# The first linear layer of the state-read tokens in seven half products

## The chip, the cores and the metric

The kernel runs on one core of a Trainium2 chip. Its time is the device time of one execution in microseconds, the median of several runs. Before the change it is 203.69 us (three runs, 203.05 to 204.18).

## The reference

The input x is 8 batches x 8 heads x 512 rows x 64, the state 8 x 8 x 32 x 64. Attention is taken both ways, and the result goes through a feed-forward layer with SILU:

```python
scores = scale * np.matmul(x, state.transpose(0, 1, 3, 2))
a = np.exp(scores); a /= a.sum(-1, keepdims=True) + 1e-09
xread = np.matmul(a, state)
scores2 = scale * np.matmul(state, x.transpose(0, 1, 3, 2))
a2 = np.exp(scores2); a2 /= a2.sum(-1, keepdims=True) + 1e-09
sread = np.matmul(a2, x)
attn = np.concatenate([xread, sread], axis=2)
# rows of attn, 512 wide (8 heads x 64), are the tokens
h = tokens @ w_in            # 512 -> 2048
out = silu(h) @ w_out        # 2048 -> 512
```

Each batch gives 544 tokens: 512 from `xread` and 32 from `sread`. The change concerns the 8 x 32 = 256 tokens of `sread`, the state-read tokens.

## The kernel before

The order of all work is written out by hand: each engine does its instructions in the order in which the code names them, and waits where an operand or a buffer isn't ready. A batch b = 0..7 has two layers. G1 gives h for 16 tiles of 128 features and ScalarE turns each into g with SILU (`emit_G1`, L549). G2 multiplies g by `w_out_sb`. From batch 1 on G2 is done by class `Unit` (L608) in seven products of half the size instead of eight (Strassen's scheme in Winograd's form): g is cut in two halves of features (lo, hi) and of tokens, `w_out_sb` in B11 to B22, and VectorE makes sums of both (`sums1` to `sums4`, D1 to D4 in `wt`). `u.mm(p, k)` is step k of 8 of product p, two matmuls of 128x256. Products 1, 6 and 5 add up in the PSUM bank `al`, and their intermediate sums are copied out (`kept[0]` by VectorE, `keep` by ScalarE); products 7, 2, 4, 3 each use the one bank `be`, which VectorE must have read before the next of them starts. POOL makes two of the sums of blocks; a block (i, c) is a quarter of the output of one batch. `out_half` stores half of it.

In the loop over batches (L906) G1 of batch b and products 1 and 7 of its G2 alternate (`early`, L924), then come products 2, 6, 4, 5, 3 (`units`, L1011), among which G1 of the next batch begins. Batch 7 has no next batch. There, the state-read tokens follow. Their attention sums were made in batches 1, 4 and 6 (`sread`) and moved by DMA to `xs`; `place_xm` (L450) brings them to `xmT`, [128, 2 halves of 128 tokens, 4 slices of the 512 inputs, 128 tokens], in 8 copies of 64x256 on VectorE (L958). Their G1 is the branch `b == B` of `emit_G1`: for each of 16 tiles of features four matmuls of 128x256 (L558) into a bank with the tag "h1", of which there are two, and a SILU of 128x256 (L568). Two tiles come ahead of product 2 (L990), the others are spread over products 6, 4, 5 and 3 (L1016). `sread_diff` (L752) then takes one difference of g on VectorE within product 3.

`sread_out_product` (L695) is G2 of the state-read tokens, again in seven products, and the end of the kernel: p1, p7, p6, p2, p5, p4, p3 with 8 matmuls of 128x256 each (p3 in two parts of 128x128 matmuls, 8 each). p1, p6 and p5 add up in one bank. Four stores leave on the queues of SP and ScalarE.

The banks of PSUM: `bank` (L77) hands out four in turn, `psH` two ("h1"), `psO` two ("o0" for `be`, "o1" for `al`). `x_f` (L109) are two buffers for x in f32, needed until the last batch of x is converted to bf16 by POOL; `x_nat` holds two tiles of 4 KB per partition.

Of the kernel before, what the change touches and what calls it, by code (L numbers as in the profile page):

```python
# [18 lines left out]
B = 8  # L19
H = 8  # L20
# [22 lines left out]
def kernel(  # L43
# [12 lines left out]

    pers = ctx.enter_context(tc.tile_pool(name="pers", bufs=1))
    xpool = ctx.enter_context(tc.tile_pool(name="xpool", bufs=2))
    xtpool = ctx.enter_context(tc.tile_pool(name="xtpool", bufs=2))
    att = ctx.enter_context(tc.tile_pool(name="att", bufs=2))  # L60
    epool = ctx.enter_context(tc.tile_pool(name="epool", bufs=6))
# [44 lines left out]
    xT = {}  # L106


    x_f = [pers.tile([128, H, 4, D], FP32, name=f"x_f{i}") for i in range(2)]  # L109

    def load_x(b, h0=0, nh=H, eng=nc.gpsimd):
        eng.dma_start(
# [45 lines left out]
    def copy(eng, dst, src):  # L158
        if eng is nc.scalar:
            nc.scalar.activation(dst, src, func=COPY, bias=0.0)  # L160
        else:
            eng.tensor_copy(dst, src)  # L162
# [337 lines left out]

    def g_tile(k):
        b, ft = divmod(k, NFT)
        if b == B:
            if ft == 0:
                gh[b, 0] = gpool.tile([128, NFT, 256], BF16, tag="g", name="g")
            gt[k] = gh[b, 0][:, ft, :]
        else:
            if ft % 8 == 0:
                gh[b, ft // 8] = gpool.tile([128, 8, 512], BF16, tag="g", name="g")
            gt[k] = gh[b, ft // 8][:, ft % 8, :]  # L510

    h_ps = {}

# [34 lines left out]

    def emit_G1(k):  # L549
        b, ft = divmod(k, NFT)  # L550
        if b < B:
            g1_half(k, 0)
            g1_half(k, 1)
            ps = h_ps.pop(k)
        else:
            ps = psH.tile([128, 512], FP32, tag="h1", name="h1")
            for kt in range(4):
                nc.tensor.matmul(  # L558
                    ps[:, 0:256],
                    w_in_sb[:, kt, ds(128 * ft, 128)],  # L560
                    xmT[:, :, kt].rearrange("p t n b -> p t (n b)"),
                    start=(kt == 0),
                    stop=(kt == 3),
                    skip_group_check=True,
                )
        n = 512 if b < B else 256
        g_tile(k)
        nc.scalar.activation(gt[k], ps[:, 0:n], func=SILU, bias=0.0)  # L568

    def G2(b, tt, ft):  # L570
        if ft == 0:
# [18 lines left out]
    def sub(eng, dst, a, c):  # L590
        eng.tensor_tensor(dst, a, c, op=SUB)  # L591

    def add(eng, dst, a, c):
        eng.tensor_tensor(dst, a, c, op=ADD)  # L594
# [97 lines left out]
            nc.sync.dma_start(out_sread[ds(512, 32), ds(4 * tt, 4), :], o[:])  # L692


    def sread_out_product():  # L695
        g = gh[B, 0]
        half = lambda e, t: g[:, ds(8 * e, 8), ds(128 * t, 128)]
        a11, a21, a12, a22 = half(0, 0), half(0, 1), half(1, 0), half(1, 1)
        t8 = lambda nm: spool.tile([128, 8, 128], BF16, tag=nm, name=nm)
        s1, s2 = t8("s1"), t8("s2")  # L700
        u1, u3 = (spool.tile([128, 256], FP32, tag=nm, name=nm) for nm in ("u1", "u3"))
        o = [o1pool.tile([128, DM], FP32, tag=f"o_s{i}", name="o_s") for i in range(2)]
        al = psO.tile([128, 256], FP32, tag="o1", name="o")

        def product(left, right, to=None, first=True, c=0, n=256):
            if to is None:
                to = bank([128, 256], FP32, "o_s")
            for k in range(8):
                nc.tensor.matmul(  # L709
                    to[:, 0:n],  # L710
                    left[:, k],
                    right[:, k, ds(c, n)],
                    start=(first and k == 0),
                    stop=(k == 7),
                    skip_group_check=True,
                )
# [35 lines left out]
    def sread_diff():  # L752
        g = gh[B, 0]
        sub(nc.vector, g[:, 0:8, 128:256], g[:, 0:8, 0:128], g[:, 0:8, 128:256])

    done = [0]

# [148 lines left out]
    for b in range(1, B):  # L906
# [25 lines left out]
        for j in range(lead, NFT):  # L932
            upto(NFT * b + j + 1)
            if j == 8:
                u.hi = gh[b, 1]
            if j == max(lead, 5):
                if b == 1:
                    t_weights((3,), 4, 4)
                    transpose_x(3)
                u.sums3(0, 4)  # L940
                if 1 < b and m + 1 < B:
                    fetch_x(m + 1)
                if b == 2:
                    for v in range(2):
                        evict_state(v, (nc.vector, nc.gpsimd)[v], 4, 4)
            if j == 9:
                u.sums3(4, 4)
                if b == 1:
                    for v in range(2):
                        evict_state(v, (nc.vector, nc.gpsimd)[v], 2, 2)  # L950
                    t_weights((2, 4), 4, 4, nc.gpsimd)
                elif n < B:
                    norm_t(n)
                    if b in SREAD_AT:
                        spread_x(n)
# [31 lines left out]
        if 2 < b < B - 1:  # L987
            out_a()
        if n == B:
            upto(NFT * B + 2)  # L990
        if b == 1:
            for hg in range(2):
                scores(2, hg)
        for k in range(8):
            u.mm(2, k)
        if b == 2:
            made = group_a()
        add(nc.vector, u.block(0, 0), u.kept[0][:], u.be[:])
# [7 lines left out]
            out_a()  # L1006
        if 1 < b and m < B:
            exps_t(m)
        step = 0

        def units(p, leads={}):  # L1011
            nonlocal step
            for k in range(8):
                u.mm(p, k)
                if n == B and (p != 6 or k > 5):
                    upto(NFT * B + 2 + (step + 1) * (NFT - 2) // 26)  # L1016
                    step += 1
                    if (p, k) == (3, 1):
                        sread_diff()
                if n < B and k in leads:  # L1020
                    upto(NFT * n + leads[k])

# [29 lines left out]

        if b > 1:
            group_b()
        units(5, {7: 1} if b > 1 else {})
        u.keep(nc.scalar, 0, 1)
        add(nc.gpsimd, u.block(1, 1), u.kept[1][:], u.block(0, 1))
# [9 lines left out]
            transpose_x(m + 1)  # L1067
        for ft in range(NFT):
            gt.pop(NFT * b + ft)
    upto(NFT * B + NFT)  # L1070
    sread_out_product()
# [1 line left out]
_INS = ['x', 'state', 'moe_w_in', 'moe_w_out']  # L1073
# [26 lines left out]
```

## Time and profile before

| | |
|---|---|
| median of three runs | 203.69 us (203.05 to 204.18) |
| the profiled execution: its time | 203.69 us |
| its span, first to last instruction | 201.9 us |
| TensorE busy | 195.3 us, 1912 matmuls |
| VectorE, ScalarE, POOL busy | 137.6, 138.2, 72.1 us |
| granted TensorE clock, mean | 0.996 of full speed |
| G1 of the state-read tokens on TensorE | 64 matmuls of 128x256, from 175.55 to 191.6 us |
| last arithmetic instruction ends | 198.37 us |

The times in the text count from the start of the span. Line numbers (L...) are those of the kernel before unless it says otherwise. A row of a group of instructions shows line, engine, operation, tiles (out<-in), shapes and count, then busy time in us and the mean length of one in ns, then the idle time ahead of them and who ended it. A row of the view in order of time shows start, length, engine, line and operation; in square brackets the idle time before it and who ended it. A matmul's length is its passage through the array; the next one starts earlier, so that prices of matmuls are taken from starts.

### The profile page before, as it was taken

The page shows a single profiled execution, that of the slowest core. Times are in us where ns is not written, and L with a number is a line of the kernel's source. Part 1 is how long each engine was busy: PE and PEld are TensorE (multiplying, and loading weights), DVE is VectorE, ACT ScalarE, POOL GpSimd, SP SyncE. Part 2 cuts the span into 40 slices and gives each one's busy share as a digit, 9 for nine tenths or more (in the row PEclk, how much of TensorE's full clock was granted, in tenths as well). Part 3 has the DMA queues.
Part 4 walks back from the last instruction along what each step waited for, and adds up shares of the span by engine and source line. Part 5 has one row for each costly group of instructions (what it writes and reads, how often), then busy time and mean ns, then how long its engine had stood idle before and what let it go on. Part 6 is the DMA issues. An engine that isn't in the chain of part 4 may idle for free.

```text
span 201.9 us, 4650 instructions
## 1 busy us (share of the span) xinstructions
PE 195.3 (97%) x1912; PEld 130.7 (65%) x1912; DVE 137.6 (68%) x244; ACT 138.2 (68%) x245; POOL 72.1 (36%) x89
## 2 busy tenths in 40 slices
PE   7899999999999999999999999999999999999992
PEld 2444335567766676667766677668666876688881
DVE  3862655977997899388947974779369955862162
ACT  2875657889767887879787957888588168724520
POOL 8673333696534702730373034323202230002200
PEclk9999999999999999999999999999999999999998
DMA  5999999995057996494239812965142005000222
GB/s 183 194 205 206 246 263 348 211 238 120 3 147 186 238 269 123 200 273 102 52 136 281 162 27 56 259 101 29 38 196 55 13 3 208 0 3 0 102 109 104
DMA packets 40965, 28.71 MB, mean 142 GB/s; under 512 B 27376, under 2 KB 37616, under 8 KB 40944
## 3 DMA queue, kind: packets, MB, share of 16 engines
q1 hardware_dynamic: 34736, 20.65, 40.5%
q0 software_dynamic: 5920, 7.64, 18.3%
q8 instruction: 15, 0.25, 0.5%
q10 hardware_dynamic: 288, 0.13, 0.2%
q14 instruction: 6, 0.05, 0.1%
HBM read 17.43 MB, written 8.91 MB: 130 GB/s over the span
## 4 chain that ended last, share of the span: by engine, by line
PE 86%; DMA 8%; POOL 2%; DVE 1%; ACT 1%; issue 1%; POOLq 0%
PE o L646 43%; PE h L540 25%; DMA x_f<-in_x_dram 8%; PE ps_w L473 4%; PE h L558 4%; PE ps_busy L168 2%; PE o_a L577 1%; PE o L709 1%; PE o_s L709 1%; PE ps_sr L420 1%; PE o L577 1%; PE ps_xt L257 1%; PE ps_scT L336 1%; POOL w_in_sb L153 1%; PE ps_sc L310 1%
## 5 line engine op out<-in xcount | busy, mean ns | idle before, releaser
L568 ACT ACTIVATE g<-h 128x512 bf16<-128x512 f32 (+1 forms) x142 | 79.9, 573 | 34.5 <-PE h L540 23.7
L646 PEld LDWEIGHTS <-g 128*128 128x128 bf16 x560 | 54.2, 98 | 29.1 <-issue 0.5
L540 PE MATMUL h<-aT,W 128*128 128x512 bf16 x252 | 72.7, 379 | 0.1
L646 PE MATMUL o<-w_out_sb,g 128*128 128x256 bf16 x336 | 48.6, 273 | 0.1
L646 PE MATMUL o<-wt,g 128*128 128x256 bf16 x224 | 33.0, 273 | 0.0
L594 POOL TENSOR_TENSOR o_sb<-o_sb,kept 128x512 f32<-128x512 f32 x7 | 11.0, 1569 | 54.8 <-ACT o_sb L160 39.6
L540 PEld LDWEIGHTS <-W 128*128 128x128 bf16 x252 | 24.4, 98 | 8.6 <-issue 0.8
L646 PE MATMUL o<-wt,s 128*128 128x256 bf16 x224 | 27.4, 273 | 0.0
L162 DVE CAST W<-ps_w 128x512 bf16<-128x512 f32 (+1 forms) x35 | 21.7, 664 | 6.3 <-PE ps_w L473 6.3
L594 DVE TENSOR_TENSOR o_sb<-o_sb,o 128x512 f32<-128x512 f32 x14 | 9.6, 682 | 24.1 <-PE o L646 20.8
L646 PEld LDWEIGHTS <-s 128*128 128x128 bf16 x224 | 21.5, 98 | 4.3 <-issue 1.7
L160 ACT ACTIVATE W<-ps_w 128x512 bf16<-128x512 f32 (+1 forms) x31 | 16.4, 583 | 5.7 <-PE ps_w L473 5.6
L162 POOL CAST x_nat<-x_f 128x512 bf16<-128x512 f32 x24 | 16.2, 716 | 6.0 <-issue 4.1
L591 DVE TENSOR_TENSOR g<-g 128x1024 bf16<-128x1024 bf16 x15 | 11.8, 784 | 9.2 <-ACT g L568 9.2
L594 POOL TENSOR_TENSOR o_sb<-kept,o_sb 128x512 f32<-128x512 f32 x7 | 8.9, 1265 | 24.1 <-ACT o_sb L160 24.1
L160 ACT ACTIVATE o_sb<-o 128x512 f32<-128x512 f32 x15 | 8.9, 595 | 10.1 <-issue 6.8
L591 DVE TENSOR_TENSOR g<-g,s 128x1024 bf16<-128x1024 bf16 x15 | 14.1, 978 | 0.0
L162 DVE COPY kept<-o 128x512 f32<-128x512 f32 x14 | 9.6, 686 | 6.2 <-PE o L646 6.0
L366 POOL TENSOR_TENSOR an<-e,rcn 128x512 bf16<-128x512 bf16 x5 | 7.7, 1534 | 15.7 <-DVE rcn L364 15.6
L591 DVE TENSOR_TENSOR s<-g 128x512 bf16<-128x512 bf16 (+3 forms) x23 | 12.5, 571 | 0.1
L473 PE MATMUL ps_w<-w_in_sb,stT 64*32 64x512 bf16 (+1 forms) x264 | 10.2, 375 | 0.3 <-DMA w_in_sb<-in_moe_w_in_dram 0.3
L577 PEld LDWEIGHTS <-g 128*128 128x128 bf16 x64 | 5.8, 98 | 7.0 <-issue 0.8
(104 smaller groups left out, 212.7 us busy)
## 6 DMA issues: line engine op xcount, KB each, us to landing
out_dram<-o_sb SPq DMA_DIRECT2D x14, 512.0 KB, 2.7
x_f<-in_x_dram SPq DMA_DIRECT2D x6, 512.0 KB, 4.6
x_f<-in_x_dram POOLq DMA_DIRECT2D x2, 1024.0 KB, 11.6
x_f<-in_x_dram SPq DMA_DIRECT2D x2, 1024.0 KB, 6.1
w_out_sb<-in_moe_w_out_dram POOLq DMA_DIRECT2D x6, 256.0 KB, 11.3
w_in_sb<-in_moe_w_in_dram POOLq DMA_DIRECT2D x3, 512.0 KB, 11.2
x_f<-in_x_dram POOLq DMA_DIRECT2D x2, 512.0 KB, 15.3
out_dram<-o_sb SPq DMA_DIRECT2D x4, 256.0 KB, 5.9
```

What stands on the lines that cost most here:

```text
L160: nc.scalar.activation(dst, src, func=COPY, bias=0.0)
L162: eng.tensor_copy(dst, src)
L168: nc.tensor.matmul(ps[:], busy[:, 0:128], busy[:], start=True, stop=True, skip_group_check=True)
L366: eng.tensor_tensor(a[:, hg], e2[b][:, hg], rc[:, hg].to_broadcast([128, 4, 4, NS]), op=MULT)
L473: nc.tensor.matmul(pss[f, hg][ds(32 * s, 32), 0:n], stT[ds(r, 64), b, h // 2, s % 2, :], w_in_sb[ds(r, 64), h // 2, ds(f, n)], start=True, ...
L540: nc.tensor.matmul(h_ps[k][:], W1[b][:, hg, ds(128 * ft, 128)], aT[b][:, hg, :, :], start=(hg == 0), stop=(hg == 1), skip_group_check=True,)
L558: nc.tensor.matmul(ps[:, 0:256], w_in_sb[:, kt, ds(128 * ft, 128)], xmT[:, :, kt].rearrange("p t n b -> p t (n b)"), start=(kt == 0), stop ...
L568: nc.scalar.activation(gt[k], ps[:, 0:n], func=SILU, bias=0.0)
L577: nc.tensor.matmul(outs[tt][:], gt[b * NFT + ft][:, ds(128 * tt, 128)], w_out_sb[:, ft, :], start=(ft == 0), stop=(ft == NFT - 1), skip_gr ...
L591: eng.tensor_tensor(dst, a, c, op=SUB)
L594: eng.tensor_tensor(dst, a, c, op=ADD)
L646: nc.tensor.matmul(to[:, t, :], left[:, ds(128 * t, 128)], right[:, k, :], start=first and t == 0, stop=(k == 7), skip_group_check=True,)
```

## The change

G1 of the state-read tokens is done in seven half products too. The 512 inputs are cut in two halves e, the 2048 features in two halves c (so that feature tiles f and f + 8 form a pair), the 256 tokens in two halves t. Class `StateReadG1` makes four sums of `w_in_sb` (S1 to S4, each bf16 128x2048, on VectorE) and four sums of `xmT` (T, 128x256). The sums of weights lie in the buffers of `x_f`, which for that move to a pool of their own.

The seven products p are done for two groups g of four feature pairs: 14 items, in the order 1, 7, 6, 4, 5, 2, 3 for each group. An item is 4 x 2 matmuls of 128x128 into one bank of [128, 4, 128]. Items 1, 6 and 5 add up in a bank `h_al`, the others have a bank each from the four of `bank`, so that item 3 comes to the bank that `h_al` has. ScalarE copies the three states of `h_al` to SBUF, VectorE copies item 7 and makes five additions of f32 128x512 per group, and ScalarE makes four SILUs of 128x512 from SBUF. The f32 pieces (s0, p7, u1, u3) take the two buffers of `x_nat`; those of the second group wait for the SILUs of the first.

Items 1 and 7 of group 0 come ahead of product 2, the other 12 are spread over the 40 steps of products 2, 6, 4, 5 and 3, about one every three steps. S3 and S1 are made in batch 6 ahead of product 5, S2 early in batch 7, the sums of `xmT` behind `place_xm`, whose second half is now copied by POOL, and S4 after the first two items. Product 3 ends, as before, ahead of the output product.

In `sread_out_product` the difference s3 (formerly `sread_diff`) is taken after p1, the order becomes p1, p2, p7, p6, p4, p5, p3, two copies change their engine, and the four stores become three (of 512, 384 and 128 columns).

```diff
-    x_f = [pers.tile([128, H, 4, D], FP32, name=f"x_f{i}") for i in range(2)]
+    x_f = [xfpool.tile([128, H, 4, D], FP32, tag=f"x_f{i}", name=f"x_f{i}") for i in range(2)]
...
     def emit_G1(k):
...
-            for kt in range(4):
-                nc.tensor.matmul(ps[:, 0:256], w_in_sb[:, kt, ds(128 * ft, 128)],
-                    xmT[:, :, kt].rearrange("p t n b -> p t (n b)"), ...)
...
+    class StateReadG1:
+        def __init__(self):
+            w = w_in_sb.rearrange("p (e k) (c f) -> p e c k f", e=2, c=2)
+            self.A = {(c, e): w[:, e, c] for e in range(2) for c in range(2)}
...
+            self.items = [(g, p) for g in range(2) for p in (1, 7, 6, 4, 5, 2, 3)]
...
+        def w_sums(self, which):   # on VectorE
+            S[1] = A[1, 0] + A[1, 1]; S[2] = S[1] - A[0, 0]
+            S[3] = A[0, 0] - A[1, 0]; S[4] = A[0, 1] - S[2]
+        def x_sums(self):          # on VectorE, X(e, t) of xmT
+            T[0] = X(0, 1) - X(0, 0); T[1] = X(1, 1) - T[0]
+            T[2] = X(1, 1) - X(0, 1); T[3] = X(1, 0) - T[1]
+            self.ops = {1: (A[0, 0], X(0, 0)), 2: (A[0, 1], X(1, 0)), 3: (S[4], X(1, 1)),
+                4: (A[1, 1], T[3]), 5: (S[1], T[0]), 6: (S[2], T[1]), 7: (S[3], T[2])}
...
+        def item(self):
+            g, p = self.items.pop(0)
+            left, right = self.ops[p]
...
+            ps = self.al if p in (1, 6, 5) else bank([128, 4, 128], FP32, "h_be")
+            for f in range(4):
+                for k in range(2):
+                    nc.tensor.matmul(ps[:, f], left[:, k, ds(128 * (4 * g + f), 128)], right[:, k], ...)
...
+            if p == 1:
+                copy(nc.scalar, s0, h)
+            elif p == 7:
+                copy(nc.vector, p7, h)
+            elif p == 6:
+                copy(nc.scalar, u1, h)
+                add(nc.vector, u1, u1, p7)
+            elif p == 4:
+                add(nc.vector, u1, u1, h)
+                self.silu(g, 1, 0, u1)
+            elif p == 5:
+                copy(nc.scalar, u3, h)
+                add(nc.vector, p7, p7, u3)
+                self.silu(g, 1, 1, p7)
+            elif p == 2:
+                add(nc.vector, s0, s0, h)
+                self.silu(g, 0, 0, s0)
+            else:
+                add(nc.vector, u3, u3, h)
+                self.silu(g, 0, 1, u3)
...
     def sread_out_product():
...
         product(a11, B11, al)
-        copy(nc.vector, o[0][:, lo], al[:])
+        sub(nc.vector, s3, a11, a21)
+        copy(nc.scalar, o[0][:, lo], al[:])
...
+        p2 = product(a12, B21)
+        add(nc.vector, o[0][:, lo], o[0][:, lo], p2[:])
         p7 = product(s3, D3)
-        copy(nc.scalar, o[1][:, hi], p7[:])
+        copy(nc.vector, o[1][:, hi], p7[:])
         product(s2, D2, al, False)
...
-        p2 = product(a12, B21)
-        add(nc.vector, o[0][:, lo], o[0][:, lo], p2[:])
-        out(0, 0, 256, nc.sync)
-        sub(nc.vector, a12, a12, s2[:])
+        p4 = product(a22, D4)
         add(nc.vector, u1[:], u1[:], o[1][:, hi])
+        sub(nc.vector, s2[:], a12, s2[:])
+        add(nc.vector, o[1][:, lo], u1[:], p4[:])
         product(s1, D1, al, False)
         copy(nc.scalar, u3[:], al[:])
         add(nc.vector, o[1][:, hi], o[1][:, hi], u3[:])
-        p4 = product(a22, D4)
-        add(nc.vector, o[1][:, lo], u1[:], p4[:])
         out(1, 0, 512, nc.sync)
-        for c, queue in ((0, nc.scalar), (128, nc.sync)):
-            p3 = product(a12, B22, c=c, n=128)
+        for c in (0, 128):
+            p3 = product(s2, B22, c=c, n=128)
             add(nc.vector, o[0][:, ds(256 + c, 128)], u3[:, ds(c, 128)], p3[:, 0:128])
-            out(0, 256 + c, 128, queue)
+            if c == 0:
+                out(0, 0, 384, nc.scalar)
+        out(0, 384, 128, nc.sync)
...
+                if n == B:
+                    rg.w_sums((2,))
...
-                        place_xm(half, nc.vector)
+                        place_xm(half, (nc.vector, nc.gpsimd)[half])
+                    rg.x_sums()
...
         if n == B:
-            upto(NFT * B + 2)
+            rg.item()
+            rg.item()
+            rg.w_sums((4,))
...
+        def sread_g1():
+            nonlocal step
+            step += 1
+            while n == B and rg.items and 12 - len(rg.items) < step * 12 // 37:
+                rg.item()
...
+        if n == B - 1:
+            rg = StateReadG1()
+            rg.w_sums((3, 1))
         units(5, {7: 1} if b > 1 else {})
```

More of the change, by code (lines that the diff above doesn't have):

```diff
@@ L58 @@
     xpool = ctx.enter_context(tc.tile_pool(name="xpool", bufs=2))
+    xfpool = ctx.enter_context(tc.tile_pool(name="xfpool", bufs=1))
     xtpool = ctx.enter_context(tc.tile_pool(name="xtpool", bufs=2))
@@ L502, in g_tile @@
         b, ft = divmod(k, NFT)
[L503 to L510, printed above, removed]
+        if ft % 8 == 0:
+            gh[b, ft // 8] = gpool.tile([128, 8, 512], BF16, tag="g", name="g")
+        gt[k] = gh[b, ft // 8][:, ft % 8, :]
     h_ps = {}
@@ L550, in emit_G1 @@
         b, ft = divmod(k, NFT)
[L551 to L556, printed above, removed]
-            for kt in range(4):
[L558 to L566, printed above, removed]
+        g1_half(k, 0)
+        g1_half(k, 1)
+        ps = h_ps.pop(k)
         g_tile(k)
-        nc.scalar.activation(gt[k], ps[:, 0:n], func=SILU, bias=0.0)
+        nc.scalar.activation(gt[k], ps[:], func=SILU, bias=0.0)
     def G2(b, tt, ft):
@@ L692, in store, with X, silu @@
             nc.sync.dma_start(out_sread[ds(512, 32), ds(4 * tt, 4), :], o[:])
+    class StateReadG1:
+        def __init__(self):
+            w = w_in_sb.rearrange("p (e k) (c f) -> p e c k f", e=2, c=2)
+            self.A = {(c, e): w[:, e, c] for e in range(2) for c in range(2)}
+            wide = [
+                xfpool.tile([128, 2, 2, 1024], BF16, tag=f"x_f{i}", name="w_s") for i in range(2)
+            ]
+            self.S = {i + 1: wide[i // 2][:, i % 2] for i in range(4)}
+            self.tx = pers.tile([128, 4, 2, 128], BF16, name="t_x")
+            self.items = [(g, p) for g in range(2) for p in (1, 7, 6, 4, 5, 2, 3)]
+            self.al = None
+            self.parts = {}
+        def w_sums(self, which):
+            A, S = self.A, self.S
+            for i in which:
+                if i == 1:
+                    add(nc.vector, S[1], A[1, 0], A[1, 1])
+                elif i == 2:
+                    sub(nc.vector, S[2], S[1], A[0, 0])
+                elif i == 3:
+                    sub(nc.vector, S[3], A[0, 0], A[1, 0])
+                else:
+                    sub(nc.vector, S[4], A[0, 1], S[2])
+        def x_sums(self):
+            def X(e, t):
+                return xmT[:, t, ds(2 * e, 2)].rearrange("p k n b -> p k (n b)")
+            T = [self.tx[:, i] for i in range(4)]
+            sub(nc.vector, T[0], X(0, 1), X(0, 0))
+            sub(nc.vector, T[1], X(1, 1), T[0])
+            sub(nc.vector, T[2], X(1, 1), X(0, 1))
+            sub(nc.vector, T[3], X(1, 0), T[1])
+            A, S = self.A, self.S
+            self.ops = {
+                1: (A[0, 0], X(0, 0)),
+                2: (A[0, 1], X(1, 0)),
+                3: (S[4], X(1, 1)),
+                4: (A[1, 1], T[3]),
+                5: (S[1], T[0]),
+                6: (S[2], T[1]),
+                7: (S[3], T[2]),
+            }
+        def silu(self, g, c, t, src):
+            nc.scalar.activation(
+                gh[B, 0][:, ds(8 * c + 4 * g, 4), ds(128 * t, 128)],
+                src.rearrange("p (f t) -> p f t", f=4),
+                func=SILU,
+                bias=0.0,
+            )
+        def item(self):
+            g, p = self.items.pop(0)
+            left, right = self.ops[p]
+            if p == 1:
+                self.al = bank([128, 4, 128], FP32, "h_al")
+                if g == 0:
+                    gh[B, 0] = gpool.tile([128, NFT, 256], BF16, tag="g", name="g")
+                two = [
+                    xpool.tile([128, 2, 512], FP32, tag="x_nat", name="h_part") for _ in range(2)
+                ]
+                self.parts = {1: two[0][:, 0], 7: two[0][:, 1], 6: two[1][:, 0], 5: two[1][:, 1]}
+            ps = self.al if p in (1, 6, 5) else bank([128, 4, 128], FP32, "h_be")
+            for f in range(4):
+                for k in range(2):
+                    nc.tensor.matmul(
+                        ps[:, f],
+                        left[:, k, ds(128 * (4 * g + f), 128)],
+                        right[:, k],
+                        start=(p in (1, 7, 4, 2, 3) and f == 0 and k == 0),
+                        stop=(k == 1),
+                        skip_group_check=True,
+                    )
+            h = ps.rearrange("p f t -> p (f t)")
+            s0, p7, u1, u3 = (self.parts[i] for i in (1, 7, 6, 5))
+            if p == 1:
+                copy(nc.scalar, s0, h)
[14 more added lines that the diff above has]
+                self.silu(g, 0, 0, s0)
+            else:
+                add(nc.vector, u3, u3, h)
+                self.silu(g, 0, 1, u3)
@@ L743, in sread_out_product @@
         add(nc.vector, o[1][:, hi], o[1][:, hi], u3[:])
-        p4 = product(a22, D4)
-        add(nc.vector, o[1][:, lo], u1[:], p4[:])
         out(1, 0, 512, nc.sync)
-        for c, queue in ((0, nc.scalar), (128, nc.sync)):
-            p3 = product(a12, B22, c=c, n=128)
+        for c in (0, 128):
+            p3 = product(s2, B22, c=c, n=128)
             add(nc.vector, o[0][:, ds(256 + c, 128)], u3[:, ds(c, 128)], p3[:, 0:128])
-            out(0, 256 + c, 128, queue)
-    def sread_diff():
-        g = gh[B, 0]
-        sub(nc.vector, g[:, 0:8, 128:256], g[:, 0:8, 0:128], g[:, 0:8, 128:256])
+            if c == 0:
+                out(0, 0, 384, nc.scalar)
+        out(0, 384, 128, nc.sync)
     done = [0]
@@ L993 @@
                 scores(2, hg)
+        step = 0
+        def sread_g1():
[3 more added lines that the diff above has]
+                rg.item()
         for k in range(8):
             u.mm(2, k)
+            sread_g1()
         if b == 2:
@@ L1008 @@
             exps_t(m)
-        step = 0
         def units(p, leads={}):
-            nonlocal step
             for k in range(8):
                 u.mm(p, k)
[L1015 to L1019, printed above, removed]
+                sread_g1()
                 if n < B and k in leads:
@@ L1069 @@
             gt.pop(NFT * b + ft)
-    upto(NFT * B + NFT)
     sread_out_product()
```

## The prediction

> **What bounds the kernel now.** I read the page first, then the chain, then the end of batch 7 by stretches, by kinds of instruction and in order of time.
>
> ```profile
> PE 195.3 (97%) x1912; PEld 130.7 (65%) x1912; DVE 137.6 (68%) x244; ACT 138.2 (68%) x245; POOL 72.1 (36%) x89
> PE 86%; DMA 8%; POOL 2%; DVE 1%; ACT 1%; issue 1%; POOLq 0%
> ```
>
> TensorE sets the time: 97% busy and 86% of the chain. The stretches show where the change falls: batch 7's products (first row), the last product and its tail (second), the end of the stores (third). Columns: microseconds, busy time by engine, granted clock, DMA share, GB/s.
>
> ```profile
> 176.50:191.40 14.90, 14.90 (x139) 13.35 (x137) 5.18 (x10) 6.46 (x17) 2.53 (x2) 1.00 0.06 24
> 191.40:198.40 7.00, 6.53 (x67) 5.53 (x64) 5.03 (x12) 1.53 (x4) 0.00 (x0) 1.00 0.31 122
> 198.40:201.90 3.50, 0.00 (x0) 0.00 (x0) 0.00 (x0) 0.00 (x0) 0.00 (x0) 0.79 0.32 112
> ```
>
> In the first TensorE never rests, while VectorE works only 5.18 of 14.9 us and ScalarE 6.46. That slack is what the change spends. Durations, by form, from 165 us on:
>
> ```profile
> L558 PE MATMUL h<-xmT,w_in_sb 128*128 128x256 bf16 x64 | 9.6, 272 | 0.0
> L162 DVE COPY xmT<-xs 64x256 bf16<-64x256 bf16 x8 | 3.0, 374 | 0.1
> L594 DVE TENSOR_TENSOR o_sb<-kept,o 128x512 f32<-128x512 f32 x1 | 0.7, 686 | 1.5 <-PE o L646 1.5
> ```
>
> And in order of time (start, length, engine), the rows whose prices or waits I use:
>
> ```profile
> 160.07 2.36 DVE L591 TENSOR_TENSOR g<-g,s 128x1024 bf16<-128x1024 bf16 x2
> 160.17 1.70 POOL L594 TENSOR_TENSOR o_sb<-o_sb,kept 128x512 f32<-128x512 f32 x1 [7.33 <-ACT o_sb L160]
> ...
> 175.55 1.23 PE L558 MATMUL h<-xmT,w_in_sb 128*128 128x256 bf16 x8
> 175.75 0.69 DVE L162 COPY kept<-o 128x512 f32<-128x512 f32 x1 [0.62 <-PE o L646]
> 178.56 0.69 DVE L594 TENSOR_TENSOR o_sb<-kept,o 128x512 f32<-128x512 f32 x1 [1.45 <-PE o L646]
> 179.17 1.28 DVE L594 TENSOR_TENSOR s<-s,g 128x1024 bf16<-128x1024 bf16 x2
> 180.37 1.28 DVE L591 TENSOR_TENSOR g<-g,s 128x1024 bf16<-128x1024 bf16 x2
> ...
> 191.46 1.04 PE L709 MATMUL o<-w_out_sb,g 128*128 128x256 bf16 x8
> ...
> 193.48 0.77 PEld L709 LDWEIGHTS <-s 128*128 128x128 bf16 x8 [0.39 <-DVE s L591]
> ...
> 196.99 1.06 PE L709 MATMUL o_s<-w_out_sb,g 128*128 128x128 bf16 x16
> ...
> 198.08 0.29 DVE L594 TENSOR_TENSOR o_s<-u,o_s 128x128 f32<-128x128 f32 x1 [0.16 <-PE o_s L709]
> ```
>
> **TensorE's own work.** Four 256-wide products of L558 start at 180.11 and the next ones at 180.54: 0.109 us each. The sixteen 128-wide ones start from 196.99 to 197.83: 0.84/15 = 0.056 each, every one with new weights. Removed: 64 x 0.109 = 6.98. Added: 7 products x 2 groups x 8 = 112 x 0.056 = 6.27. Gain 0.71. The first two old tiles spread over 1.23 us, because they waited for the two "h1" banks; the new items take their own banks, gain 0.16. The gap of 0.39 before 193.48 (plus 0.07 of handover) goes if p2, moved ahead of p7, covers the differences. Ideal gain 1.3 us before the last store.
>
> The Trainium skill ("TensorE: Matmul & The Clock Gate", section on LDWEIGHTS) gives 128 columns of weights an estimated 128/1.2 = 107 ns, which speaks against halving the width; by it alone the 112 would take 12.0 us, 5.0 more than the old 64, instead of 0.71 less. The sixteen at 0.056 in this trace decide: the load does not bind here.
>
> **What VectorE and ScalarE get.** Each group adds on VectorE one PSUM copy and five f32 additions of 128x512, on ScalarE three copies and four SILUs of 512. By the 178.56 and 179.17 rows such a VectorE operation lasts 0.69 and the next starts 0.61 after it; 0.72 if it needs its result. SBUF-only f32 has no 512 row; 256 took 0.420 from SBUF alone and 0.421 with PSUM, so the same 0.69. Two groups: 12 x 0.61 + 4 x 0.1 for dependent ones = about 7.5 us. S4 (bf16 128x2048) is 1.21 by the one such row, wt of L591. The removed difference of the read was 0.69. From kept[1] at 175.75 to the last addition VectorE now has some 13.6 us of work (these 7.5, S4, and the s, g and block operations that it had); without stalls TensorE would finish the last item at 189.9, 14.2 us after that start, so every wait shows. ScalarE: 6 copies and 8 SILUs at 0.60 (two in a row take 1.08), for sixteen at 0.38: it has the time, but its queue is in order.
>
> Handovers, from the same rows: a reader starts 0.2 after the last product's slot; otherwise 0.05.
>
> **POOL and VectorE exclude each other** when VectorE reads two SBUF tensors: the pair at 160.07 takes 2.36, the same pair at 180.37 without POOL 1.28, and POOL's addition 1.70 instead of 1.26. I read this as one waiting out the other.
>
> I then walked the queues with these prices, in the recorded order of the changed program.
>
> *Before 176.* VectorE is free from 164.22. S3 runs 164.26 to 165.48; POOL's addition waits for it (to 166.66) and S1 for POOL (to 167.88). S2, the two differences of g, and four xmT copies on POOL then alternate. POOL has no 64x256 row: its 64x64 copies take 0.38, 64x128 0.49, so 0.70 by the slope; below, VectorE's 0.374. I take 0.55, between them, since both rows may hold waiting. VectorE's four copies end at 174.0, the four x sums (0.285 each) at 175.15, kept[0] at 175.76, the first s2 at 176.37, kept[1] at 176.98 instead of 176.44. Product 2 needs that bank: it starts at 177.02 instead of 176.44, where two items end. Price 0.58; 0.04 with POOL at 0.374.
>
> *Group 0.* VectorE runs without a rest to 181.32 (item 4's addition ends at 180.72); then ScalarE's SILU and, behind it, the copy of item 5 end at 181.86, after 0.59 of rest. TensorE isn't held. Additions to 183.80, s1 to 185.02. keep of block (1,0), behind three SILUs, ends at 184.95; POOL's addition at 186.25, and the second pair of g differences waits for it: 186.25 to 187.55. Block (1,0)'s addition ends at 188.16.
>
> *Group 1.* Only then come items 6 and 4: u1 is complete at 189.48. Its SILU ends at 190.12 and the copy of item 5, queued behind it though its product ended at 188.24, at 190.62. Item 3 reuses that bank: it starts at 190.67 instead of 189.99, price 0.68. The last three additions end at 192.56; ScalarE finishes the SILU of item 5 at 191.99, keep of (0,1) at 192.49, the last two SILUs at 193.49. p1 needs the bank that keep reads, and starts at 192.54 where its queue would have let it at 191.76: 0.78. POOL's last addition runs 192.54 to 193.80; VectorE's addition into block (0,1) must wait for it (to 194.53), and the difference s3, queued behind that, ends at 195.14. TensorE has done p1 and p2 by 194.35 (0.07 lost inside p1), and p7 starts at 195.18: 0.83 lost.
>
> *The tail.* p7, p6, p4, p5 at 0.87 and p3 at 0.89 end at 199.56; u3's copy now comes after p5, directly ahead of p3, so the last addition ends at 200.13 (0.57 behind the products; 0.49 before). Against 198.37: +1.76. Check: 0.58 + 0.68 + 0.78 + 0.07 + 0.83 = 2.94, less the ideal 1.3, plus 0.08 = 1.72, and rounding.
>
> *Stores.* Before, SP sent 256 KB at 197.7, ScalarE 64 KB at 197.95, SP 64 KB at 198.40 after 128 KB had left at 195.9; data moved from 198.87 to 200.15. Now 256, 192 and 64 KB leave within 0.6 us. SP's issue of 0.54 holds the last back by at least 0.2; the extra 128 KB at the 300 GB/s of that burst would cost 0.4 more, partly beside. I take +0.2; bounds 0 and 0.75.
>
> Sum: 1.76 + 0.2 = about +1.95. The profiled run took 203.69 with a span of 201.9, and is the median of the three; so 205.6.
>
> **Rivals.**
> 1. VectorE keeps ahead and TensorE sets the pace (other side). For: 13.6 us fit into 14.2 if nothing waits. p1 starts at 190.55, products end at 196.67, the last addition at 197.24; with 0.2 for the stores -0.9: 202.8, and from 202.6 to 203.3 with stores from 0 to 0.75. Against: the ScalarE queue puts SILUs ahead of copies that free banks. The point: if an f32 512 operation cost 0.42 between starts instead of 0.61, the walk's last addition comes at 198.25, even with before. 0.22.
> 2. The exclusion of POOL and VectorE does not reach these operations. Without any, the walk ends at 199.08, +0.7, with stores +0.9: 204.6. With POOL's copies at 0.374 alone it is 199.59, +1.4: 205.1, which I count to the forecast. 0.09.
> 3. New weights every 128 columns, beside 256-wide products, cost more than in the last product. At 0.109 each the walk's last addition comes at 203.93: with the stores +5.8, 209.5. Against: the sixteen at 0.056. 0.03.
> 4. The change does not shorten TensorE's list at all: excluded, the recorded order has the 112 products for the 64.
>
> **Numbers.** Forecast 0.63, own range 204.9 to 206.7 (POOL at 0.374; f32 operations 5% longer, last addition at 200.57, and stores at 0.75); something worse that I haven't seen, 0.03. The range 203.0 to 206.8 holds the forecast, rival 2 and about half of rival 1: 0.63 + 0.09 + 0.11 = 0.83. 0.5% is 1.0 us, about what a measurement can tell here: within 202.7 to 204.7. Faster: the lower end of rival 1, 0.08. Same: its rest and half of rival 2, 0.19. Slower: 0.73.
>
> **What would show it.** Right: VectorE near 13.5 us busy from 176 to 192; ScalarE idle for over 2 us before item 4's SILU in group 1, and TensorE idle before item 3 of group 1; p1 held by keep, p7 by s3 behind POOL. Wrong: TensorE unbroken from 175.5 to the last product, or products of the items slower than 0.45 us each. VectorE's f32 additions shorter than 0.69 or a shorter POOL copy would break the size, not the kind.

## The result

The changed kernel takes 205.84 us (median of four runs, 204.76 to 207.15), the one before 203.37 on the same chip: a ratio of 1.0118, 95% interval 1.0072 to 1.0164. It is slower by 1.2%. The forecast was 205.6 with a range of 203.0 to 206.8. The span of the profiled run is 204.0 us (201.9 before).

The page's busy times after the change, then the first and the last of the stretches that the prediction showed (the last is the end of the stores, which lies later here):

```profile
PE 194.7 (95%) x1960; PEld 130.9 (64%) x1960; DVE 153.1 (75%) x260; ACT 140.1 (69%) x243; POOL 77.8 (38%) x93
```

```profile
176.50:191.40 14.90, 14.29 (x178) 13.13 (x176) 12.75 (x20) 6.95 (x13) 1.27 (x1) 1.00 0.01 2
...
200.40:204.00 3.60, 0.00 (x0) 0.00 (x0) 0.00 (x0) 0.00 (x0) 0.00 (x0) 0.99 0.40 146
```

TensorE has less to do (194.7 for 195.3) and rests where it never did. VectorE went from 5.18 to 12.75 us busy in the stretch of batch 7's products; ScalarE only from 6.46 to 6.95, and yet it is ScalarE that TensorE waits for. The order of time shows how, with start, length, engine, and in brackets the idle time and who ended it:

```profile
175.71 0.69 DVE L163 COPY kept<-o 128x512 f32<-128x512 f32 x1 [0.17 <-PE o L629]
176.45 1.03 PE L629 MATMUL o<-w_out_sb,g 128*128 128x256 bf16 x8
...
188.33 0.69 DVE L577 TENSOR_TENSOR h_part<-h_part,h_be 128x512 f32<-128x512 f32 x1
188.78 0.82 PE L629 MATMUL o<-w_out_sb,g 128*128 128x256 bf16 x6
189.05 0.63 ACT L724 ACTIVATE g<-h_part 128x512 bf16<-128x512 f32 x1 [2.72 <-DVE h_part L577]
189.59 0.58 ACT L161 ACTIVATE h_part<-h_al 128x512 f32<-128x512 f32 x1
190.20 0.69 DVE L577 TENSOR_TENSOR h_part<-h_part 128x512 f32<-128x512 f32 x1 [1.18 <-ACT h_part L161]
190.22 0.61 PE L745 MATMUL h_be<-xmT,w_s 128*128 128x128 bf16 x8 [0.61 <-ACT h_part L161]
190.66 0.82 PE L629 MATMUL o<-w_out_sb,g 128*128 128x256 bf16 x6
...
191.46 0.58 ACT L161 ACTIVATE o_sb<-o 128x512 f32<-128x512 f32 x1
192.09 1.14 PE L790 MATMUL o<-w_out_sb,g 128*128 128x256 bf16 x8 [0.61 <-ACT o_sb L161]
192.12 1.27 POOL L577 TENSOR_TENSOR o_sb<-kept,o_sb 128x512 f32<-128x512 f32 x1 [6.24 <-ACT o_sb L161]
...
193.42 0.69 DVE L577 TENSOR_TENSOR o_sb<-o_sb,o 128x512 f32<-128x512 f32 x1 [1.34 <-POOL o_sb L577]
194.02 0.68 DVE L574 TENSOR_TENSOR g<-g 128x1024 bf16<-128x1024 bf16 x1
...
194.76 1.05 PE L790 MATMUL o_s<-wt,g 128*128 128x256 bf16 x8 [0.67 <-DVE g L574]
...
199.23 0.48 DVE L577 TENSOR_TENSOR o_s<-u,o_s 128x128 f32<-128x128 f32 x2
```

ScalarE sits idle for 2.72 us until VectorE has finished u1 (item 4 of group 1), and the copy that empties the bank for item 3 is behind that SILU in its queue. That copy's product, item 5, starts at 187.23; in the first experiment below, where nothing stands ahead of it, the copy starts 0.64 after its product's start. So it could have run from about 187.87 on, but starts at 189.59. TensorE's idle time in brackets counts from the modelled end of the last matmul; by starts, the loss is larger: six matmuls from 188.78 at 0.109 end their slots at 189.43, and item 3 starts at 190.22, 0.79 later. In the same way 0.78 is lost ahead of p1 (190.66 + 0.65 = 191.31, start 192.09) and 0.83 ahead of p7 (p2 starts at 193.06).

In the profiled runs the first item (or tile) starts between 174.79 and 175.55, so they differ by up to 0.8 us in what lies ahead of it. They are therefore compared from the start of the first item (first tile in the kernel before) to the end of the last addition, and from there to the end of the span, which is known to 0.1:

| | first item to last addition | from there to the end |
|---|---|---|
| before | 22.82 (175.55 to 198.37) | 3.53 |
| after | 24.21 (175.50 to 199.71) | 4.29 |

The change loses 1.39 us in the arithmetic and 0.76 in the stores.

### The profile page after: what moved, and what is told of

Read it like the earlier page. It is cut to its first block, busy times and chain, and to the rows that moved or that the text cites. A ratio compares the mean times of both kernels' runs of the same rounds, so it can differ in the third digit from the quotient of the medians.

```text
span 204.0 us, 4777 instructions
## 1 busy us (share of the span) xinstructions
PE 194.7 (95%) x1960; PEld 130.9 (64%) x1960; DVE 153.1 (75%) x260; ACT 140.1 (69%) x243; POOL 77.8 (38%) x93
## 5 line engine op out<-in xcount | busy, mean ns | idle before, releaser
L551 ACT ACTIVATE g<-h 128x512 bf16<-128x512 f32 x126 | 73.7, 597 | 25.3 <-PE h L536 23.0
L574 DVE TENSOR_TENSOR g<-g 128x1024 bf16<-128x1024 bf16 x15 | 12.3, 818 | 6.8 <-ACT g L551 6.8
L574 DVE TENSOR_TENSOR s<-g 128x512 bf16<-128x512 bf16 (+3 forms) x23 | 11.3, 520 | 0.1
```

The costliest lines, as they stand in the source:

```text
L551: nc.scalar.activation(gt[k], ps[:], func=SILU, bias=0.0)
```

## The experiments

All ratios are to the kernel before, with 95% intervals. Each is the changed kernel with one edit, unless it says otherwise.

**The copy ahead of the SILU.** ScalarE's order alone.

```diff
             elif p == 4:
                 add(nc.vector, u1, u1, h)
-                self.silu(g, 1, 0, u1)
             elif p == 5:
                 copy(nc.scalar, u3, h)
+                self.silu(g, 1, 0, u1)
```

> The changed kernel with one exchange on ScalarE: the copy of item 5 stands ahead of the SILU of item 4 instead of behind it, in both groups. Theory, order of ScalarE's queue: item 3 of group 1 waited 0.61 us for a bank whose copy stood behind a SILU that waited for VectorE. The wait goes, VectorE's rest of 1.18 ahead of the third addition of group 1 goes too, keep of block (0,1) and with it p1, POOL's addition and s3 move up by about 1.0: span 202.9 to 203.2. Rival, sheer work of VectorE: its 13.6 us set the end, so the wait only moves to another place, and the span falls by under 0.3, to 203.7 or more.

Measured: 204.04 us, ratio 1.0011 (0.9988 to 1.0035), which can't be told from the kernel before. First item to last addition 22.66, 1.55 less. In the order of time of this kernel:

```profile
187.77 0.60 ACT L161 ACTIVATE h_part<-h_al 128x512 f32<-128x512 f32 x1 [1.54 <-PE h_al L745]
188.68 1.23 ACT L724 ACTIVATE g<-h_part 128x512 bf16<-128x512 f32 x2 [0.31 <-DVE h_part L577]
...
189.33 0.61 PE L745 MATMUL h_be<-xmT,w_s 128*128 128x128 bf16 x8
189.78 0.82 PE L629 MATMUL o<-w_out_sb,g 128*128 128x256 bf16 x6
...
190.45 1.13 PE L790 MATMUL o<-w_out_sb,g 128*128 128x256 bf16 x8
```

The copy waits only for its product, item 3 and p1 have no idle time, and TensorE goes without a break to the end of p2. VectorE's work is the same, so its amount alone didn't hold TensorE there; the order of ScalarE's queue did. The wait ahead of p7 is left, 0.83 as before. The theory gave 1.0 and got 1.55: it had counted that keep moves up, but not that both waits, 0.79 and 0.78, would go whole.

**VectorE's work made less.** The same question from the other side.

```diff
+        if n == B - 2:
+            rg = StateReadG1()
+            rg.w_sums((3, 1))
         if n == B - 1:
-            rg = StateReadG1()
-            rg.w_sums((3, 1))
+            rg.w_sums((2, 4))
...
-                if n == B:
-                    rg.w_sums((2,))
...
             rg.item()
             rg.item()
-            rg.w_sums((4,))
```

> The changed kernel with the four sums of weights one place earlier: S3 and S1 in batch 5, S2 and S4 in batch 6, so that 1.21 us of VectorE's work go from the stretch of the items and 1.21 from that ahead of it, and nothing of what ScalarE does is changed. Theory, order of the queues: behind the copy of item 7 VectorE then rests until ScalarE has copied item 6 (178.57), 0.1 before it starts now; first item to last addition falls by 0.1 to 0.3, to 23.9 to 24.1. Rival, sheer work of VectorE: it falls by about 1.1, to 23.1.

Measured: 205.68 us, ratio 1.0089 (1.0056 to 1.0121); first item to last addition 24.09, 0.12 less. In its order of time VectorE waits where S4 used to be:

```profile
177.78 0.60 ACT L161 ACTIVATE h_part<-h_al 128x512 f32<-128x512 f32 x1 [1.22 <-PE h_al L745]
178.41 0.69 DVE L577 TENSOR_TENSOR h_part<-h_part 128x512 f32<-128x512 f32 x1 [0.93 <-ACT h_part L161]
```

1.2 us less work for VectorE gave a tenth of that, because VectorE spends most of what it gained there waiting for ScalarE. Its sheer amount of work is not what sets the end; what less work behind this wait would give, this run doesn't show.

**The additions left out.**

```diff
             elif p == 6:
                 copy(nc.scalar, u1, h)
-                add(nc.vector, u1, u1, p7)
             elif p == 4:
-                add(nc.vector, u1, u1, h)
                 self.silu(g, 1, 0, u1)
...
-                add(nc.vector, p7, p7, u3)
...
-                add(nc.vector, s0, s0, h)
...
-                add(nc.vector, u3, u3, h)
```

> The changed kernel without the ten f32 additions of the items on VectorE; the SILUs read the bare copies, so the state-read tokens' result is left out in part (the sums of products), while all products, copies and SILUs stay. Theory: TensorE itself gained, and only VectorE's additions and what waits for them lost it. Then no stall is left ahead of item 3, p1 or p7, p1 starts at 190.5 to 190.7, the last addition ends near 197.3, and the span is 201.3 to 201.8 with the later stores (4.3 behind), so just under the kernel before. Rival, the 128-wide products cost more than 0.056 among 256-wide ones: p1 starts at 191.5 or later even so, and the span is 202.3 or more.

Measured: 202.95 us, ratio 0.9961 (0.9936 to 0.9986); p1 starts 15.03 us after the first item (174.89 to 189.92), first item to last addition 21.71, end 4.30 behind it. There is no stall of TensorE left. In the kernel before p1 starts 15.91 behind the first tile: TensorE does gain 0.88 here, so the rival of dearer 128-wide products falls. The additions took VectorE's work and the SILUs' wait for VectorE with them, so this run doesn't tell work from order.

**s3 ahead of the last block.**

```diff
+        if n == B:
+            g = gh[B, 0]
+            sub(nc.vector, g[:, 0:8, 128:256], g[:, 0:8, 0:128], g[:, 0:8, 128:256])
         add(nc.vector, u.block(0, 1), u.block(0, 1), u.be[:])
         u.out_half(0)
...
         product(a11, B11, al)
-        sub(nc.vector, s3, a11, a21)
```

> The changed kernel with the difference s3 on VectorE ahead of the last addition into block (0,1), which waits for POOL, instead of behind it. Theory: p7 waits for s3, and s3 stood behind that addition; s3 now needs the last SILU (193.08) and the end of POOL's addition (193.39), because both read two SBUF tensors: it runs about 193.4 to 194.1, p7 starts at 194.1 instead of 194.76, and the span falls by 0.6 to 203.4. If POOL and VectorE didn't exclude each other, s3 would run from 193.1 and p7 start at 193.95 directly behind p2: 0.8 less. Rival: p7 is held by the SILU alone and nothing changes (204.0).

Measured: 204.98 us, ratio 1.0060 (1.0022 to 1.0098); first item to last addition 23.62, 0.59 less, as expected. POOL and s3 in the order of time:

```profile
191.39 1.28 POOL L577 TENSOR_TENSOR o_sb<-kept,o_sb 128x512 f32<-128x512 f32 x1 [6.24 <-ACT o_sb L161]
...
192.39 0.83 DVE L574 TENSOR_TENSOR g<-g 128x1024 bf16<-128x1024 bf16 x1 [1.03 <-ACT g L724]
...
193.28 0.94 PE L790 MATMUL o_s<-wt,g 128*128 128x256 bf16 x7
```

s3 lasts 0.83 instead of 0.68, and ends 0.55 after POOL's addition does (192.67), although nothing of POOL's is its operand. p7 now starts 0.07 behind p2's slots (192.34 + 0.87 = 193.21, start 193.28) where it was 0.83, which alone would give 0.76. But s2, the difference that p6 reads, now stands behind the addition into the block, and p6 starts 1.06 after p7 (194.34) instead of 0.89. So 0.17 came back, which the theory had not; that the sum is the expected 0.6 is in part chance.

**The four stores of before.**

```diff
         add(nc.vector, o[0][:, lo], o[0][:, lo], p2[:])
+        out(0, 0, 256, nc.sync)
...
-            if c == 0:
-                out(0, 0, 384, nc.scalar)
-        out(0, 384, 128, nc.sync)
+            out(0, 256 + c, 128, (nc.scalar, nc.sync)[c > 0])
```

> The changed kernel with the four stores of the kernel before (256 columns behind p2's addition, then 512, 128 and 128) in place of its three. In the changed kernel the end of the span lies 4.3 us behind the last addition (199.71 to 204.0), before it was 3.5 (198.37 to 201.9). Theory, the burst: 512 KB leave within 0.8 us instead of 384, and the last store waits for them. Then the distance falls back to 3.5 to 3.7, the span by 0.6 to 0.8 us to 203.2 to 203.4, and the stalls of TensorE ahead of item 3, p1 and p7 (0.61, 0.61, 0.67) stay. Rival, the order of the additions: the last store is late because the addition that frees the 512 columns now comes directly ahead of it and SP issues one store at a time; then the distance stays at 4.1 or more.

Measured: 205.15 us, ratio 1.0066 (1.0041 to 1.0090). First item to last addition 24.20, unchanged; the end 3.87 behind it: 0.42 less, but 0.34 more than before the change. So the burst is only a part of it, and neither the theory's 3.5 to 3.7 nor the rival's 4.1 was met.

**The new output product alone**, in the kernel before: order, engines of the copies and stores as in the diff of the change, s3 taken early as `sread_diff` does.

> The kernel before with the new output product alone: its order p1, p2, p7, p6, p4, p5, p3, its engines for the copies and its three stores; G1 stays in full products and the difference s3 is taken early as before. Theory: the gap of 0.39 and the handover of 0.07 ahead of p6 go, the last addition stands 0.08 later behind the products, so first item to last addition falls from 22.82 to 22.4; the end lies 4.3 instead of 3.5 behind it, so that the new order alone costs 0.3 to 0.4: 204.0. Rival, the long distance to the end in the changed kernel comes from the state in which G1 leaves the queues: then it stays at 3.5 here and the kernel gains 0.4.

Measured: 204.01 us, ratio 1.0022 (0.9995 to 1.0050). First tile to last addition 22.59, 0.23 less, where 0.42 was expected; the end 4.30 behind it. The long distance belongs to the new order and its stores, not to the new G1. The products run unbroken, but the gap had been worth less: p7 of the kernel before starts at 192.34 and ends its slots at 193.21, p6 starts at 193.48, 0.27 and not 0.46.

**xmT on VectorE.** `place_xm(half, nc.vector)` for both halves.

> The changed kernel with both halves of xmT copied by VectorE, as before the change, instead of the second half by POOL. POOL's four copies took 0.98 to 1.62 us each, and VectorE's operations beside them 2.28, 1.64, 1.11 instead of 1.21, 1.21, 0.69. Theory (the forecast's step): these waits hold VectorE back, but at 175.71 it had caught up, so the first wait ahead of product 2 was worth 0.0 to 0.1. With the copies on VectorE it has 1.5 more to do there and about 2 less to wait: no change, first item to last addition 24.1 to 24.3. If VectorE then comes late to kept, product 2 starts later and the span is longer by what it is late, up to 0.8.

Measured: 205.94 us, ratio 1.0108 (1.0077 to 1.0139); first item to last addition 24.38, 0.17 more. kept[1] is copied 0.45 us after the first item starts, in the changed kernel 0.21. Product 2 starts 1.19 after the first item instead of 0.95. So POOL's share helps a little in the profile, in spite of the waits; the times, 205.94 and 205.84, can't tell the two kernels apart.

**Three edits together**: copy first, s3 first, four stores.

> Three edits at once on the changed kernel: the copy of item 5 ahead of the SILU of item 4, s3 ahead of the last addition into block (0,1), and the four stores of the kernel before. Each alone moved, from the first item to the last addition or from there to the end: 1.55, 0.59 and 0.42 us. Theory, the three losses are separate: 24.21 falls to 22.0 to 22.2 from the first item to the last addition (22.82 before), the distance behind it is 3.8 to 3.9 (3.53 before), so the kernel is 0.3 to 0.6 us faster than the one before: 203.0 to 203.3 where that takes 203.6. Rival, the two waits share their cause (the queue of ScalarE), and behind the first edit the second has little left: 22.6, and 203.7.

Measured: 202.91 us, ratio 0.9969 (0.9945 to 0.9994), faster than both kernels; first item to last addition 22.09, end 3.87 behind it. The waits ahead of item 3, p1 and p7 are gone or nearly so:

```profile
188.87 0.61 PE L745 MATMUL h_be<-xmT,w_s 128*128 128x128 bf16 x8
189.32 0.82 PE L629 MATMUL o<-w_out_sb,g 128*128 128x256 bf16 x6
189.99 1.13 PE L790 MATMUL o<-w_out_sb,g 128*128 128x256 bf16 x8
190.96 1.04 PE L790 MATMUL o_s<-w_out_sb,g 128*128 128x256 bf16 x8
191.89 1.05 PE L790 MATMUL o_s<-wt,g 128*128 128x256 bf16 x8
192.36 0.75 DVE L574 TENSOR_TENSOR s<-g 128x768 bf16<-128x768 bf16 x2
192.96 0.77 PEld L790 LDWEIGHTS <-s 128*128 128x128 bf16 x8 [0.30 <-DVE s L574]
```

By starts TensorE still loses 0.36: 0.10 inside p1, 0.06 ahead of p7 and 0.20 ahead of p6, whose weights are s2 (p7's slots end at 191.89 + 0.87 = 192.76, p6 starts at 192.96). 1.55 and 0.59 add up to 2.14, measured 2.12: the losses were separate. Two more kernels then took up the 0.34 that was left in the stores.

**Queues of the last two stores exchanged**, on the combined kernel: `(nc.sync, nc.scalar)[c > 0]`.

> The combined kernel with the queues of its last two stores exchanged: the 128 columns of the first part of p3 on SP, behind the 512, and the last 128 columns on ScalarE's queue, which is free. In the combined kernel the end lies 3.87 behind the last addition, 0.34 more than in the kernel before, although the stores are of the same sizes. Theory, SP issues one store in 0.55 to 0.65 us and the last store waits 0.2 for the one of 512 columns: it now leaves 0.03 behind the last addition, the distance falls to 3.6 to 3.7. Rival, the amount still to be moved at the end (320 KB sent within 0.6 us): 3.8 to 3.9, no change.

Measured: 202.63 us, ratio 0.9946 (0.9913 to 0.9980), but the end lies 3.88 behind the last addition, as in the combined kernel. This does not decide between SP's issue and the amount, because the exchange didn't take SP's wait away: now the store of the first 128 columns is behind the 512 on SP, and it is issued at 197.49, 0.27 behind the last addition's end (197.22). In the combined kernel the last store on SP is issued 0.27 behind it too (197.30, 197.03).

**The large store in two halves**, on the combined kernel.

```diff
         add(nc.vector, o[1][:, lo], u1[:], p4[:])
+        out(1, 0, 256, nc.sync)
...
-        out(1, 0, 512, nc.sync)
+        out(1, 256, 256, nc.sync)
...
-            out(0, 256 + c, 128, (nc.scalar, nc.sync)[c > 0])
+        out(0, 256, 256, nc.scalar)
```

> The combined kernel with its 512-column store in two of 256, the first as soon as p4's addition is done (0.8 us earlier), and the two 128-column stores as one of 256 on ScalarE's queue behind the last addition. The amount to be moved behind u3's addition falls from 384 to 256 KB, and no store waits for SP. Theory, amount and SP's issue both: the distance from the last addition to the end falls from 3.87 to about 3.5, the kernel by 0.3 to 202.6. Rival, the end is set by the last store alone, and 128 KB in it take longer than 64: 3.8 or more.

Measured: 202.45 us, ratio 0.9961 (0.9937 to 0.9984); first item to last addition 22.09 again, the end 3.44 behind it. What is sent from u3's addition on was 512 KB in the changed kernel, 384 in the combined one, 256 here; the distance 4.29, 3.87, 3.44. What the end waits for is seen in the DMA engines' busy tenths from 196 to 204 us, 0.2 us a digit, in the kernel before, the changed, the combined and this one:

```profile
DMA  0000008910000059998840000000000000000000
DMA  9899100000000000000000069999996000000000
DMA  0000000005998992000000000000000000000000
DMA  0000004950395880000000000000000000000000
```

In the first three the engines are busy at eight or nine tenths from the first of these bytes (198.8, 200.6, 197.8) to the last, and the span ends some 1.8 us later. A last store that was issued sooner would have found them busy. So by these rows, though by no experiment, the end hangs on when the first large store leaves and on the bytes, 0.42 us for the 128 KB between the changed and the combined kernel. In the kernel before, 384 KB were still to come as in the combined one, but the store of 256 KB had left 0.68 us ahead of the last addition's end (197.69 to 198.37), and in the combined kernel only 0.37 (196.66 to 197.03): that is about the other 0.34. In this kernel the digits dip to 5 at 198.4: the last store, issued 0.04 behind the last addition, finds the engines nearly free, and the end hangs on it alone. That the step is 0.43 once more is therefore partly chance.

This is the fastest of the kernels by its median, the one before it by its ratio; the intervals of the last three overlap.

## Why the prediction was right, and where it was not

The forecast held: slower, 205.6 against 205.84, with the span longer by 2.1 where the sum gave 1.95. The signs that it named are all there: VectorE 13.85 us busy from 176 to 192, ScalarE idle for 2.72 ahead of item 4's SILU, TensorE idle ahead of item 3, p1 held by keep and p7 by s3. So the mechanism behind the larger part of the loss was right. But two of the terms were wrong by about as much, in opposite directions, and that the sum came out so close is luck.

1. *TensorE's own work*, -0.71: right. An item of eight takes 0.44 (182.83 to 183.27), and the combined kernel, with no stall from product 2 to p1, reaches p1 15.05 after the first item instead of 15.91: 0.86 less, for 0.71 and 0.16. The forecast's third gain, 0.46 for the gap ahead of p6, was 0.27 to 0.30 on TensorE: I had read the idle time of the weight loads and not the starts of the matmuls.

2. *Before 176*, 0.58: wrong, it was about 0.05 (product 2 starts 0.95 after the first item, two items take 0.89). The step that failed is when VectorE comes to kept[1]. The forecast had it 0.54 late. It was done with the x sums at 174.33 instead of 175.15, had time to spare, and waited 0.17 for product 7 before it copied kept[1] at 175.71.

```profile
165.23 2.28 DVE L577 TENSOR_TENSOR w_s<-w_in_sb 128x2048 bf16<-128x2048 bf16 x1
...
166.38 5.41 POOL L163 COPY xmT<-xs 64x256 bf16<-64x256 bf16 x4
...
168.04 0.68 DVE L574 TENSOR_TENSOR g<-g 128x1024 bf16<-128x1024 bf16 x1
168.64 1.64 DVE L574 TENSOR_TENSOR w_s<-w_s,w_in_sb 128x2048 bf16<-128x2048 bf16 x1
```

The exclusion and the alternation are there as forecast: S1 took 2.28 for 1.21 beside POOL's addition, POOL's copies 1.35 each, and S2, which starts while POOL's second copy (168.06 to 169.20) is under way, 1.64 for 1.21. The times were not: S1 was done at 167.51 instead of 167.88, and POOL's first copy (to 168.00) ran beside VectorE's addition at 167.44, which has an operand in PSUM and took its usual length, 0.67. So the first difference of g, at 168.04 just ahead of POOL's second copy, waited for nothing. How the rest of the 0.82 splits can't be said, since the forecast gave no times in between. The lower bound that it gave, 0.04, was close to the value.

3. *Group 1* and *the tail*: the mechanism and the sizes were right. Item 3: 0.68 forecast, 0.79 measured. p1: 0.78 and 0.78, with 0.07 and 0.10 inside it (192.09 to 193.06, against 0.87). p7: 0.83 and 0.83. Sum 2.50; less the gains of 0.71, 0.16 and 0.30, plus 0.06 for the last addition behind the products: 1.39, as measured. The experiments show each cause: item 3 and p1 hang on the copy behind the SILU (both waits go with that one exchange), p7 on s3 behind the addition that waits for POOL (0.83 falls to 0.07).

4. *Stores*, 0.2 with bounds 0 and 0.75: mis-sized, 0.76. Of this 0.42 is the extra 128 KB in the burst, which the forecast had priced at 0.4 and then took as hidden "partly beside" other work; nothing hid it. The rest, 0.34, is about the head start that the store of 256 KB lost. SP's issue, the reason given for the 0.2, does not show as the cause, since the DMA engines were busy throughout; no run tried it alone.

Rival 1, VectorE keeping ahead, did not occur, for the reason held against it, the order of ScalarE's queue. With that order and the place of s3 mended it nearly does occur: the combined kernel. The point that the forecast named, shorter additions, was not tried; without any additions TensorE has no stall either, while less work for VectorE ahead of them changed little.

Rival 2, no exclusion, is refuted by S1 beside POOL's addition (2.28 for 1.21) and by the second pair of g differences (1.78 at 185.25, beside POOL's addition from 184.60 to 185.87, where the kernel before took 1.28 for it). The Trainium skill states this rule ("SBUF — State Buffer", section "Who interferes with whom"): a VectorE operation with two SBUF inputs contends with a GpSimd operation that reads SBUF, over ports that the two share and that one locks for itself. S1 and s3 agree: each ends later than POOL's addition by its own length alone less 0.13 (1.08 and 0.55 us).

Rival 3, weights reloaded every 128 columns, is refuted by the items of 0.44. The skill's estimate of 107 ns per weight load is near the 98 ns that the trace gives one load, but the loads overlap and the matmuls start every 0.056 us, so it is not what an item costs. The same page, "TensorE: Matmul & The Clock Gate", says in its lines on queue depths that ScalarE and VectorE are strictly first in, first out. This case agrees: for the last 1.2 of the 2.72 us that ScalarE waited for VectorE, a copy was ready behind the SILU and did not run.

## What to carry to other kernels

When work is moved from a full engine to ones with slack, walk their queues in order and look for an instruction that frees a buffer behind one that waits for a third engine; exchanging two such lines gave back 1.55 of 2.15 us here, while 1.2 us less work, at a place that a wait followed, gave 0.12. Price what is still to be stored when the last arithmetic ends by its bytes, as long as the DMA engines are busy to the end (0.42 us per 128 KB here), and send large blocks as soon as they are whole. A forecast that comes out right in the sum is to be checked term by term: here errors of 0.5 and 0.6 in opposite directions cancelled.

## What was not expected of the hardware

VectorE's operations and POOL's four copies took turns in the order in which they started (POOL's at 166.38, 168.06, 169.26 and 170.81). S2 and the second difference of g, which started while one of POOL's copies was under way, ended 1.08 and 0.54 us after it, which is their own length alone less 0.13 and 0.14.

Not expected was that the first of VectorE's four xmT copies, which has a single SBUF input, did the same: it started at 171.24 and took 0.789 while POOL's last copy ran to 171.79, where the others took 0.374 to 0.379. Why it waited was not tried.
